# Weaving two GEMMs and the attention of the next batch step by step, with all tails on 128 rows

## Chip, cores and metric

The kernel runs on one core of a Trainium2 chip. The metric is the device time in microseconds (us). TensorE (PE) does the matmuls, VectorE (DVE) and ScalarE (ACT) read its results out of the PSUM banks (an eviction), and GpSimd (POOL) issues the input loads.

## The reference

For each of 8 batches, a Nystrom attention runs over 8 heads of 576 tokens and 64 features, followed by two GEMMs with a squared relu between them.

```python
q_lm, k_lm = segment means of q, k        # 32 segments of 18 tokens
A, Bm, C = softmax(q k_lm^T), softmax(q_lm k_lm^T), softmax(q_lm k^T)
for _ in range(6): Z = 2 * Z - Z @ Bm @ Z # Newton, 32x32 per head
x = A @ Z @ C @ v                         # per head, heads joined: 4608 x 512
out = relu(x @ w_in)**2 @ w_out           # 512 -> 2048 -> 512
```

The kernel folds Z, C, v and w_in into one matrix G per batch. The first GEMM is therefore A times G ("mlp_in", 64 matmuls of 288 columns a batch), and the second is "mlp_out" (576 matmuls of 512 columns in all). The products that make G are called W products below. The first W product of a batch marks the end of its attention.

## The kernel before

576 tokens are four chunks of 128 and a tail of 64. Before, each tail is a matmul whose stationary operand has 64 rows:

```python
for c in range(NC4 + 1):
    r = P if c < NC4 else TAIL                      # 128, or 64 for the tail
    nc.tensor.matmul(means[:, (1 - ti) * NPAIR + p, :],
        lhsT=X[nm][0:r, c, 2*p:2*p+2, :].rearrange("p h d -> p (h d)"),
        rhs=seg[0:r, c, :], start=(c == 0), stop=(c == NC4))
# ... the same pattern in the transposes of q, k and A, and in C times v
```

`batch_loads` loads q, k and v of a batch and copies q and k into another layout on VectorE. Batch 1 is loaded after w_out. The list scheduler of the language orders the instructions of each engine before the run, by its own estimate of when data is ready. The engines then keep that order.

```python
loaded[0] = batch_loads(0)           # ... w_in, constants, w_out (cut) ...
loaded[1] = batch_loads(1)
# inside batch_loads:
nc.vector.tensor_copy(nat[:, 0:NC4, :, :], raw.rearrange("p h c d -> p c h d"))
# main loop
res = {0: attention(0)}
for b in range(B):
    if b + 2 < B: loaded[b + 2] = batch_loads(b + 2)
    if b + 1 < B: res[b + 1] = attention(b + 1)
    mlp_in(b, *res.pop(b), gT)
    for t in tiles_of(b): mlp_out(b - b % 2, t, gT)   # same batch; one PSUM bank "o"
```

The Newton loop ran the two groups of four heads one after the other. It had separate copies and updates of 128 and 256 columns for each.

The softmax here doesn't subtract the row's maximum and nothing guards it: scores larger than these inputs give would overflow.

Of the kernel before, what the change touches and what calls it, by code (L numbers as in the profile page):

```python
# [8 lines left out]
P = 128  # L9
# [7 lines left out]
B = 8  # L17
H = 8
S = 576
D = 64  # L20
# [13 lines left out]
def kernel(  # L34
# [15 lines left out]
    small = ctx.enter_context(tc.tile_pool(name="small", bufs=3))  # L50
    newt = ctx.enter_context(tc.tile_pool(name="newt", bufs=4))
# [6 lines left out]
    def batch_loads(b: int):  # L58

        X = {}  # L60
        for nm, src in (("k", k), ("q", q)):
            raw = loads.tile([P, H, NC4, D], BF16, tag="raw")
            nat = loads.tile([P, NC4 + 1, H, D], BF16, tag=nm + "nat")
            nc.gpsimd.dma_start(
                raw[:], src[b, :, 0:NC4 * P, :].rearrange("h (p c) d -> p h c d", c=NC4)
            )
            nc.gpsimd.dma_start(
                nat[0:TAIL, NC4, :, :], src[b, :, NC4 * P:S, :].rearrange("h p d -> p h d")
            )
            nc.vector.tensor_copy(  # L70
                nat[:, 0:NC4, :, :], raw.rearrange("p h c d -> p c h d")
            )
            X[nm] = nat
        vm = loads.tile([P, H, NC4, D], BF16, tag="vm")
        vt = loads.tile([P, H, D], BF16, tag="vt")
        nc.gpsimd.dma_start(
            vm[:], v[b, :, 0:NC4 * P, :].rearrange("h (p c) d -> p h c d", c=NC4)
        )
        nc.gpsimd.dma_start(
            vt[P - TAIL:P, :, :], v[b, :, NC4 * P:S, :].rearrange("h p d -> p h d")  # L80
        )
        X["vm"], X["vt"] = vm, vt
        return X

    loaded = {}
    loaded[0] = batch_loads(0)
    for j in range(4):
        nc.gpsimd.dma_start(
            w_in_bf[:, :, j * 512:(j + 1) * 512],
            moe_w_in[:, j * 512:(j + 1) * 512].rearrange("(kt cp) f -> cp kt f", cp=P),  # L90
        )

    ident_bf = const.tile([P, P], BF16, name="ident_bf")
    make_identity(nc, ident_bf[:])
# [5 lines left out]
    seg_f = const.tile([P, NC4 + 1, M], F32, name="seg_f")  # L100
# [3 lines left out]
    band(seg_f[:, NC4, :], [[-SEG, M]], NC4 * P, 1)  # L104
    band(seg_f[:, NC4, :], [[SEG, M]], SEG - 1 - NC4 * P, -1)
    seg = const.tile([P, NC4 + 1, M], BF16, name="seg")
    nc.vector.tensor_copy(seg[:], seg_f[:])  # L107

# [8 lines left out]

    bds = []
    for i in range(2):
        bd_t = const.tile([P, 2 * NPAIR, 2 * M], BF16, name="bd%d" % i)  # L120
        nc.vector.memzero(bd_t[:])
        bds.append(bd_t)
    EA = const.tile([P, 2, NC4 + 1, P], F32, name="EA")
    nc.vector.memset(EA[:, :, NC4, :], 1.0)

    for j in range(4):
        nc.gpsimd.dma_start(
            w_out_bf[:, 4 * j:4 * j + 4, :],
            moe_w_out[512 * j:512 * j + 512, :].rearrange("(ft fp) c -> fp ft c", fp=P),
        )  # L130
    loaded[1] = batch_loads(1)

    def acol(b, c):

        if b % 2 == 0:
            return c * P
        return 0 if c == NC4 else TAIL + c * P

    def attention(b: int):
        X = loaded.pop(b)  # L140
        BD = bds[b % 2]

        means = psum.tile([P, 2 * NPAIR, M], F32, tag="n", bufs=3)
        for ti, nm in enumerate(("k", "q")):
            for p in range(NPAIR):
                for c in range(NC4 + 1):
                    r = P if c < NC4 else TAIL
                    nc.tensor.matmul(  # L148
                        means[:, (1 - ti) * NPAIR + p, :],
                        lhsT=X[nm][0:r, c, 2 * p:2 * p + 2, :].rearrange("p h d -> p (h d)"),  # L150
                        rhs=seg[0:r, c, :],
                        start=(c == 0), stop=(c == NC4),
                    )
        nc.scalar.copy(BD[0:64, :, 0:M], means[0:64, :, :])
        nc.vector.tensor_copy(BD[64:128, :, M:2 * M], means[64:128, :, :])
        STk = small.tile([P, NPAIR, M], BF16, tag="STk")
        nc.scalar.copy(STk[:], means[:, NPAIR:2 * NPAIR, :])

        bm = psum.tile([P, 2, M], F32, tag="n", bufs=3)
        for p in range(NPAIR):  # L160
            nc.tensor.matmul(bm[64 * (p % 2):64 * (p % 2) + 64, p // 2, :],
                             lhsT=BD[:, p, :], rhs=STk[:, p, :], start=True, stop=True)
        Eb = small.tile([P, 2, M], F32, tag="Eb")
        nc.scalar.activation(Eb[:], bm[:], AF.Exp, scale=SCALE)
        rs = small.tile([P, 2], F32, tag="rs")
        nc.vector.reduce_sum(rs[:], Eb[:], axis=AX.X)
        rr = small.tile([P, 2], F32, tag="rr")
        nc.vector.reciprocal(rr[:], rs[:])
        Bn = small.tile([P, 2, M], F32, tag="Bn")
        nc.vector.tensor_tensor(Bn[:], Eb[:], rr[:, :].unsqueeze(2).to_broadcast([P, 2, M]),  # L170
                                ALU.mult)
        BnT = small.tile([P, 2, M], F32, tag="BnT")
        nc.vector.transpose(BnT.rearrange("p a m -> p (a m)"), Bn.rearrange("p a m -> p (a m)"))
        colps = psum.tile([P, 2, M], F32, tag="n", bufs=3)
        nc.tensor.matmul(colps.rearrange("p a m -> p (a m)"),
                         lhsT=blk.rearrange("p a m -> p (a m)"),
                         rhs=Bn.rearrange("p a m -> p (a m)"), start=True, stop=True)
        n1 = small.tile([P, 2], F32, tag="n1")
        nc.vector.reduce_max(n1[:], colps[:], axis=AX.X)
        c1 = small.tile([P, 2], F32, tag="c1")  # L180
        nc.vector.tensor_scalar(out=c1[:], in0=n1[:], scalar1=1e-6, scalar2=None, op0=ALU.add)
        rc = small.tile([P, 2], F32, tag="rc")
        nc.vector.reciprocal(rc[:], c1[:])

        def spread(t, qd):
            return t[:, qd, :].unsqueeze(1).to_broadcast([P, 4, M])

        sts, BTs = [], []
        for qd in range(2):
            BT = small.tile([P, 4, M], BF16, tag="BT")  # L190
            nc.vector.tensor_tensor(BT[:], spread(BnT, qd), blk[:], ALU.mult)
            st = newt.tile([P, 2, 4, M], BF16, tag="st")
            nc.vector.scalar_tensor_tensor(out=st[:, 0, :, :], in0=spread(BnT, qd),
                                           scalar=rc[:, qd:qd + 1], in1=blk[:],
                                           op0=ALU.mult, op1=ALU.mult)
            nc.vector.scalar_tensor_tensor(out=st[:, 1, :, :], in0=spread(Bn, qd),
                                           scalar=rc[:, qd:qd + 1], in1=blk[:],
                                           op0=ALU.mult, op1=ALU.mult)
            BTs.append(BT.rearrange("p a m -> p (a m)"))
            sts.append(st.rearrange("p z a m -> p (z a m)"))  # L200


        T = {}
        for nm in ("q", "k"):
            tT = attn.tile([P, NPAIR, S], BF16, tag=nm + "T", bufs=1)
            for p in range(NPAIR):
                tps = psum.tile([P, S], BF16, tag="n", bufs=3)
                for c in range(NC4 + 1):
                    r = P if c < NC4 else TAIL
                    nc.tensor.transpose(  # L210
                        tps[:, c * P:c * P + r],
                        X[nm][0:r, c, 2 * p:2 * p + 2, :].rearrange("p h d -> p (h d)"),
                        ident_bf[0:r, 0:r],
                    )
                if p % 2 == 0:
                    nc.vector.tensor_copy(tT[:, p, :], tps[:])
                else:
                    nc.scalar.copy(tT[:, p, :], tps[:])  # L218
            T[nm] = tT


        EC = attn.tile([P, 2, NC4, P], BF16, tag="EC")
        ECt = attn.tile([P, 2, P], BF16, tag="ECt")
        for nm, slot0 in (("q", NPAIR), ("k", 0)):
            for qd in range(2):
                sc = psum.tile([P, NC4, P], F32, tag="n", bufs=3)
                for i in range(2):
                    p = 2 * qd + i
                    for c in range(NC4):
                        nc.tensor.matmul(sc[:, c, 64 * i:64 * i + 64],  # L230
                                         lhsT=T[nm][:, p, c * P:c * P + P],
                                         rhs=BD[:, slot0 + p, :], start=True, stop=True)
                dst = EA[:, qd, 0:NC4, :] if nm == "q" else EC[:, qd, :, :]
                nc.scalar.activation(dst, sc[:], AF.Exp, scale=SCALE)  # L234
        tl = psum.tile([P, 2, P], F32, tag="n", bufs=3)
        for nm, slot0, r0 in (("q", NPAIR, 0), ("k", 0, P - TAIL)):
            for p in range(NPAIR):
                nc.tensor.matmul(tl[r0:r0 + TAIL, p // 2, 64 * (p % 2):64 * (p % 2) + 64],
                                 lhsT=T[nm][:, p, NC4 * P:S],
                                 rhs=BD[:, slot0 + p, :], start=True, stop=True)  # L240
        nc.scalar.activation(EA[0:TAIL, :, NC4, :], tl[0:TAIL, :, :], AF.Exp, scale=SCALE)
# [168 lines left out]
```

## Time and profile before

The median of the runs is 398.1 us.

The first view is the page of the kernel before: span, busy time of each engine, then TensorE and its granted clock in 40 slices, in tenths.

```profile
span 397.2 us, 6929 instructions
...
PE 345.4 (87%) x2768; PEld 195.7 (49%) x2768; DVE 213.7 (54%) x524; ACT 170.0 (43%) x377; POOL 46.2 (12%) x68
...
PE   0440679999999999999999999999999999999985
...
PEclk9999999999999999999999999999999999999999
```

TensorE looks full after the start, but overlapping matmuls count as busy. The Trainium skill ("Perfetto Trace Analysis", Identifying the Most-Contended Engine) says that matmul busy time is not a good measure of the distance to the limit. So I count matmuls instead. Back to back, a 512-column matmul starts every 216 ns, a 288-column one every 122 ns, a 128-column one every 56 ns.

The second view is the chain of work that ended last (start, duration in us, what). Only the first W products of batches are kept, without those of batches 2 and 3.

```profile
58.72 1.96 PE g L326 x6
...
95.63 0.77 PE g L326 x6
...
220.87 0.77 PE g L326 x6
...
264.99 0.77 PE g L326 x6
...
306.30 0.77 PE g L326 x6
...
350.42 0.77 PE g L326 x6
```

The first batch is through at 58.7 us. Steady batches then take 41.3 and 44.1 us in turn.

The third view is the timeline of the start, with the idle time before an instruction and what ended it in brackets.

```profile
37.68 0.69 DVE L70 COPY nat<-raw 128x2048 bf16<-128x2048 bf16 x1 [16.21 <-DMA raw<-in_k_dram]
38.29 0.81 DVE L216 COPY tT<-tps 128x576 bf16<-128x576 bf16 x2
...
38.79 1.44 PE L230 MATMUL sc<-bd_120,tT 128*128 128x64 bf16 x24 [14.18 <-DVE tT L216]
```

VectorE stood 16 us before the copy of batch 1's k. Batch 0's own transposed q and k stood behind that copy, so TensorE waited 14.2 us for them.

The fourth view is the timeline around fifteen transposes of a steady batch. Three of them are 64-row tails, which the timeline merges with the others.

```profile
197.09 1.44 PE L210 MATMUL tps<-ident_bf,nat 128*128 128x128 bf16 x15
...
198.46 0.66 PE L342 MATMUL h<-AT,G 128*128 128x288 bf16 x4
```

Fifteen transposes take 1.37 us from first start to the next group. At 56 ns each they would take 0.84 us.

The fifth view is TensorE's waits longer than 0.15 us (engine, line, what it waited for: us in total, times, longest).

```profile
PE sc L230 <- DVE tT L216: 14.2, 1, 14.2
PE means L148 <- DVE seg L107: 12.8, 1, 12.8
PE ops L352 <- DVE o_sb L358: 4.9, 8, 0.8
```

The first is the wait for the transposed q and k. The second, for a constant, comes before any data is there. The third is the wait for the single output bank of the second GEMM.

### The profile page before, as it was taken

The numbers are of one execution on the slowest core, as the hardware profiler recorded it, in microseconds if no ns is written. First come the engines' busy times: TensorE is split into PE (matmuls) and PEld (weight loads), VectorE is DVE, ScalarE is ACT, GpSimd is POOL, SyncE is SP. The second block draws the span as 40 slices with busy tenths as digits, with TensorE's granted clock in tenths as the row PEclk, the third lists the DMA queues.
The fourth block names the chain that finished last, engine by engine and source line by source line (L and its number), as shares of the span: only waits on it lengthen the run. The fifth ranks groups of instructions, "written<-read, shape, count | busy, mean of one in ns | idle before, by whom it ended". The sixth has DMA issues, their size and how long they took to land.

```text
span 397.2 us, 6929 instructions
## 1 busy us (share of the span) xinstructions
PE 345.4 (87%) x2768; PEld 195.7 (49%) x2768; DVE 213.7 (54%) x524; ACT 170.0 (43%) x377; POOL 46.2 (12%) x68
## 2 busy tenths in 40 slices
PE   0440679999999999999999999999999999999985
PEld 0330334754565455654565456545655556645532
DVE  1311744787179714893489426972578236952500
ACT  1020404772178313852385225832584129633500
POOL 8431220111011100210030101010000000000000
PEclk9999999999999999999999999999999999999999
DMA  9999994195228521916154613043000010002021
GB/s 105 198 206 199 189 113 57 10 111 83 59 40 108 56 85 54 103 18 115 53 56 66 100 48 58 4 45 95 28 2 22 32 54 29 2 26 81 0 79 54
DMA packets 47136, 28.23 MB, mean 71 GB/s; under 512 B 13824, under 2 KB 42496, under 8 KB 47104
## 3 DMA queue, kind: packets, MB, share of 16 engines
q0 software_dynamic: 41856, 18.35, 37.9%
q1 hardware_dynamic: 5248, 9.44, 6.4%
q8 instruction: 21, 0.34, 0.4%
q14 instruction: 11, 0.09, 0.1%
HBM read 36.70 MB, written 9.44 MB: 116 GB/s over the span
## 4 chain that ended last, share of the span: by engine, by line
PE 70%; DMA 10%; ACT 9%; DVE 4%; issue 4%; POOL 2%; DVEq 0%; ACTq 0%; POOLq 0%
PE ops L352 31%; PE h L342 15%; DMA raw<-in_q_dram 7%; PE tps L210 6%; PE g L326 5%; PE means L148 4%; DMA w_in_bf<-in_moe_w_in_dram 4%; PE cv L300 3%; ACT r L346 3%; PE nt L253 2%; DVE stn L259 2%; DVE o_sb L358 2%; ACT EA L234 2%; ACT EC L234 2%; PE tps L285 2%
## 5 line engine op out<-in xcount | busy, mean ns | idle before, releaser
L352 PE MATMUL ops<-w_out_bf,gT 128*128 128x512 bf16 x576 | 148.3, 381 | 6.3 <-DVE o_sb L358 4.9
L342 PE MATMUL h<-AT,G 128*128 128x288 bf16 x512 | 92.3, 292 | 2.4 <-ACT r L346 1.6
L346 ACT ACTIVATE r<-h 128x576 bf16<-128x576 f32 x128 | 81.3, 658 | 12.5 <-PE h L342 11.9
L352 PEld LDWEIGHTS <-gT 128*128 128x128 bf16 x576 | 53.6, 98 | 65.3 <-issue 17.8
L347 DVE TENSOR_TENSOR gT<-r 128x576 bf16<-128x576 bf16 x128 | 55.0, 450 | 16.5 <-ACT r L346 15.6
L342 PEld LDWEIGHTS <-G 128*128 128x128 bf16 x512 | 44.8, 98 | 20.8 <-issue 8.4
L358 DVE COPY o_sb<-ops 128x512 f32<-128x512 f32 x20 | 13.8, 692 | 65.6 <-PE ops L352 65.0
L331 ACT CAST G<-g 128x512 bf16<-128x512 f32 x32 | 18.1, 587 | 51.9 <-PE g L326 51.9
L210 PE MATMUL tps<-ident_bf,nat 128*128 128x128 bf16 (+1 forms) x320 | 33.4, 225 | 0.1
L148 PE MATMUL means<-seg,nat 128*128 128x32 bf16 (+1 forms) x320 | 22.4, 184 | 12.8 <-DVE seg L107 12.8
L252 ACT CAST U<-nt 128x128 bf16<-128x128 f32 x96 | 23.5, 269 | 18.8 <-PE nt L250 17.7
L218 ACT COPY tT<-tps 128x576 bf16<-128x576 bf16 x32 | 20.4, 638 | 24.5 <-PE tps L210 24.5
L356 ACT COPY o_sb<-ops 128x512 f32<-128x512 f32 x16 | 9.4, 586 | 47.1 <-PE ops L352 30.3
L333 DVE CAST G<-g 128x512 bf16<-128x512 f32 x32 | 22.1, 692 | 13.5 <-PE g L326 13.5
L210 PEld LDWEIGHTS <-nat 128*128 128x128 bf16 (+1 forms) x320 | 24.4, 102 | 9.9 <-issue 1.6
L148 PEld LDWEIGHTS <-nat 128*128 128x128 bf16 (+1 forms) x320 | 18.1, 99 | 19.7 <-DVE nat L70 8.3
L70 DVE COPY nat<-raw 128x2048 bf16<-128x2048 bf16 x16 | 11.6, 737 | 28.4 <-DMA raw<-in_k_dram 22.1
L259 DVE SCALAR_TENSOR_TENSOR stn<-stn,nt 128x256 bf16<-128x256 bf16 x64 | 24.8, 417 | 1.4 <-ACT U L252 0.5
L250 PE MATMUL nt<-stn,BT 128*128 128x128 bf16 x80 | 17.9, 224 | 5.9 <-DVE stn L259 3.7
L326 PE MATMUL g<-w_in_bf,WT 128*64 128x512 bf16 x128 | 21.7, 421 | 0.5 <-DVE WT L318 0.5
L253 PEld LDWEIGHTS <-U 128*128 128x128 bf16 x96 | 9.3, 97 | 21.8 <-ACT U L252 17.5
L230 PEld LDWEIGHTS <-tT 128*128 128x128 bf16 x256 | 10.8, 101 | 16.4 <-issue 15.1
(138 smaller groups left out, 341.4 us busy)
## 6 DMA issues: line engine op xcount, KB each, us to landing
out_dram<-o_sb SPq DMA_DIRECT2D x32, 256.0 KB, 2.3
raw<-in_k_dram POOLq DMA_DIRECT2D x8, 512.0 KB, 6.1
raw<-in_q_dram POOLq DMA_DIRECT2D x8, 512.0 KB, 7.9
vm<-in_v_dram POOLq DMA_DIRECT2D x8, 512.0 KB, 6.3
w_in_bf<-in_moe_w_in_dram POOLq DMA_DIRECT2D x4, 512.0 KB, 13.7
w_out_bf<-in_moe_w_out_dram POOLq DMA_DIRECT2D x4, 512.0 KB, 17.7
out_dram<-o_sb SPq DMA_DIRECT2D x8, 128.0 KB, 3.9
nat<-in_k_dram POOLq DMA_DIRECT2D x8, 64.0 KB, 3.2
```

Source lines behind the costliest of these rows:

```text
L148: nc.tensor.matmul(means[:, (1 - ti) * NPAIR + p, :], lhsT=X[nm][0:r, c, 2 * p:2 * p + 2, :].rearrange("p h d -> p (h d)"), rhs=seg[0:r, c ...
L210: nc.tensor.transpose(tps[:, c * P:c * P + r], X[nm][0:r, c, 2 * p:2 * p + 2, :].rearrange("p h d -> p (h d)"), ident_bf[0:r, 0:r],)
L218: nc.scalar.copy(tT[:, p, :], tps[:])
L252: nc.scalar.copy(U[:], nt[:, 0:P])
L259: nc.vector.scalar_tensor_tensor(out=stn[:], in0=st, scalar=2.0, in1=nt[:, P:3 * P], op0=ALU.mult, op1=ALU.subtract)
L326: nc.tensor.matmul(g[64 * i:64 * i + 64, :], lhsT=WT[:, 2 * qd + i, :], rhs=w_in_bf[:, 2 * qd + i, n * 512:n * 512 + 512], start=True, sto ...
L333: nc.vector.tensor_copy(dst, g[:])
L342: nc.tensor.matmul(h[:, j, 0:HALF], lhsT=G[:, qd, f * P:(f + 1) * P], rhs=AT[:, qd, j * HALF:(j + 1) * HALF], start=(qd == 0), stop=(qd == 1))
L346: nc.scalar.activation(r.rearrange("p (j t) -> p j t", j=2), h[:, :, 0:HALF], AF.Relu)
L347: nc.vector.tensor_tensor(gT[:, f, o:o + S], r[:], r[:], ALU.mult)
L352: nc.tensor.matmul(ops[:], lhsT=gT[:, f, t * P:t * P + P], rhs=w_out_bf[:, f, :], start=(f == 0), stop=(f == NF - 1))
L358: nc.vector.tensor_copy(o_sb[:], ops[:])
```

## The change

The change makes the attention a generator that yields after every step. Each first-GEMM unit is followed by a step of attention and a few matmuls of the second GEMM, which lags one batch. Tails of q and k share one 128-row chunk. Zero rows in the constants stand in for the missing half. Both Newton groups go through one copy and one update, with scores, row sums and C values woven between. Batch 1 is loaded ahead of w_out. The layout copies of q and k move from the load helper, called for batch 1 ahead of batch 0's attention, to the head of their own batch's attention. The tiles of the last second GEMM alternate between two banks. The core of the diff:

```diff
-            nat = loads.tile([P, NC4 + 1, H, D], BF16, tag=nm + "nat")
+        X["qkt"] = loads.tile([P, H, D], BF16, tag="qkt", name="qkt")
+        for nm, src, r0 in (("k", k, TAIL), ("q", q, 0)):   # k rows 64..127, q rows 0..63
...
-                    r = P if c < NC4 else TAIL
-                        lhsT=X[nm][0:r, c, 2 * p:2 * p + 2, :].rearrange("p h d -> p (h d)"),
-                        rhs=seg[0:r, c, :],
+                    src = nat[nm][:, c, 2*p:2*p+2, :] if c < NC4 else X["qkt"][:, 2*p:2*p+2, :]
+                        rhs=seg[:, c + (ti if c == NC4 else 0), :],
...
+    load_qk(1, loaded[1])
+    load_v(1, loaded[1])
     for j in range(4):                                      # w_out
...
-    loaded[1] = batch_loads(1)
...
+            nc.scalar.copy(U[:], nu[:])                     # both groups, 256 columns
+            yield
+            if side: side.pop(0)(); yield                   # scores, tails, A rows, C values, A^T
...
+        for u in range(2 * NF):
+            if u % 2 == 0: mlp_in(b, u // 2, AT, G, gT)
+            else: advance(tiles, per)                       # mlp_out of batch b - 1
+            advance(att, want - done)                       # attention of batch b + 1
```

## The prediction

> **What bounds it now.** One core, full clock throughout (clock row 9s). The overview gives TensorE 345 of 397 us busy, but matmuls overlap there, so I counted start-to-start times in the timeline. Back to back a 128x512 matmul takes 216 ns, 128x288 takes 122, 128x128 takes 56, 64 columns 29, 32 columns 25. The Trainium skill ("TensorE: Matmul & The Clock Gate", Part 1) gives N/2.4 GHz + 2.5 ns; the trace agrees. Charging each matmul that, one batch needs about 33 us of TensorE (second GEMM 15.5, first GEMM 7.8, attention about 10), 34 with the pairs of 64-column products of the W step. By the chain, a steady batch takes 41.3 and 44.1 us in turn (265 to 350 us), mean 42.7, so some 8.5 us per batch are not streaming. About 3.7 of these are the 64-row matmuls: a 128-row transpose costs 56 ns, one followed by a 64-row one 152, and leaving it 132; segment means pay 108 and 119 instead of 25. The rest is Newton waits (ACT copy, DVE update), waits for the eviction of the single output bank (6.3 us in all, groups view) and column-group switches.
>
> The start is latency: first means at 12.8 us, TensorE idle 14.2 us (waits view: scores on DVE copy), because a DVE copy of batch 1's k stands in front and its load lands at 37.5 us, behind w_out. First W product at 58.7 us, second batch's at 95.6. After the last attention: 43.6 us, partly ACT-bound.
>
> **What the change does.**
> 1. 64-row matmuls go (shared tail chunk, zero rows elsewhere). Worth 3.7 us x 6 to 7 batches on the path: 22-26 us.
> 2. Batch 1's q, k, v load ahead of w_out. The program order still puts batch 1's copies in front of batch 0's Newton updates on DVE. From before's landings (about 0.185 MB/us) k1 lands near 26, q1 near 30 us, so the 14 us wait nearly vanishes. Means still start near 12.3 us, as the mask cast stands behind q's copy. With A rows, C values and transposes inside the Newton chain, first W product near 38.5 us.
> 3. Stage 0 (attention 1 with first GEMM alone) is latency- and DVE-bound: DVE about 27 us of work. Second W product near 69 us (before 95.6).
> 4. Stages 1-6: PE 34 us. Stalls I expect left: between U product and its consumers the order holds 0.5-0.9 us of other TensorE work in several iterations, against about 0.8 us for the ACT copy plus queueing; output bank turnover about 0.3-0.8 us a tile; DVE near 75-80% occupied. I take 3 us of stalls: 37 us a batch, 222 us.
> 5. Stage 7 (first GEMM 7 with second GEMM 6): 23.5 us. Final second GEMM with alternating banks: 5 x 3.45 + 4 drain = 21.5.
>
> Sum 69 + 222 + 23.5 + 21.5 = 336 span, plus 1.4 us as before: 337.
>
> **Prediction: 337 us, 8 in 10 between 324 and 351. Faster by over 2%: 0.97; within 2%: 0.02; slower: 0.01.**
>
> **What would show it.** No 64-row groups; transposes 56 ns apart throughout; first W product 36-41 us; second 65-72; a period of 35-39 us; in the waits view Newton waits and output-bank waits dominate; the last second GEMM alone from about 314 us.
>
> **What would make it wrong.** The DVE queue (row reduce and normalise of A, 1.5 us each) stalling every Newton update: period 40, total 355. Batch 1's loads late: start 10 us longer. Weaving hiding everything: period 34.5, total 322.

## The result, and the profile after

The changed kernel takes 326.7 us (median of 4 runs, 326.4 to 327.3) against 398.1 us. All outputs are right. The ratio is 0.821, with a 95% interval of 0.819 to 0.823. A ratio is the mean time of one kernel's runs over that of the other's of the same rounds, so it is not quite the ratio of the medians.

The page of the changed kernel, same parts:

```profile
span 324.8 us, 6593 instructions
...
PE 292.1 (90%) x2662; PEld 180.7 (56%) x2704; DVE 207.5 (64%) x457; ACT 165.8 (51%) x313; POOL 46.8 (14%) x70
...
PE   0385599999999999999999999999999999999994
...
PEclk9999789999999999999999999999999999999999
```

The chain of the changed kernel, first W products of the batches, without those of 4 and 5:

```profile
39.00 1.96 PE n L381 x8
...
67.36 0.84 PE n L381 x6
...
95.18 0.83 PE n L381 x6
...
130.96 0.77 PE n L381 x5
...
237.73 0.82 PE n L381 x6
...
273.61 0.77 PE n L381 x5
```

The first batch is through at 39.0 us, 19.7 us earlier, and a steady batch takes 35.7 us ((273.61 - 130.96) / 4) instead of 42.7 ((350.42 - 179.55) / 4; batch 3's first W product came at 179.55 us).

VectorE's timeline at the start of the changed kernel shows batch 1's copy again in front of batch 0's work:

```profile
28.26 0.69 DVE L154 COPY nat<-raw 128x2048 bf16<-128x2048 bf16 x1 [3.30 <-DMA raw<-in_k_dram]
28.87 0.68 DVE L350 SCALAR_TENSOR_TENSOR st<-st,n 128x512 bf16<-128x512 bf16 x1
```

It stands further back, in front of batch 0's third Newton update, and costs VectorE 3.3 us instead of 16.2.

TensorE's timeline, one group of transposes at the start and one in a steady batch:

```profile
13.22 1.01 PE L178 MATMUL n<-ident_bf,nat 128*128 128x128 bf16 x8
...
212.68 0.61 PE L178 MATMUL n<-ident_bf,nat 128*128 128x128 bf16 x8
213.13 1.03 PE L416 MATMUL ops<-w_out_bf,gT 128*128 128x512 bf16 x4
```

In the steady batch eight transposes take 0.45 us, 56 ns each, with no 64-row matmul among them. Eight at 13 us lie 106 ns apart, although the page's clock row shows a 9 there. I come back to that.

TensorE's waits in the changed kernel:

```profile
PE n L161 <- DVE seg L106: 12.1, 1, 12.1
PE n L333 <- DVE st L350: 4.8, 6, 3.1
PE n L343 <- ACT U L336: 1.6, 5, 0.5
...
PE ops L416 <- ACT o_sb L422: 0.8, 3, 0.4
```

**One account for all kernels.** I split each profiled span into four parts. "First W" is the time of the first W product. "Needed" adds up all later matmuls of the built program at their back-to-back rate (216 ns for 512 columns, 216 for a pair of W products, 122 for 288, 109 for 256, 56 for 128, 29 for 64, 25 below). "Over" is what TensorE took beyond that, up to its last matmul. The remainder, 4 us, is the last copy and store. "Needed" takes its counts from the program, so records missing from a trace don't distort it. The median is of all runs, the other columns are of the one profiled execution.

| kernel | median us | first W | needed | over |
|---|---|---|---|---|
| before | 398.1 | 58.7 | 258.1 | 76.2 |
| before_load1 | 397.3 | 58.2 | 258.1 | 75.3 |
| before_pool12 | 390.1 | 42.9 | 258.1 | 82.7 |
| before_rows128 | 366.9 | 57.9 | 258.6 | 44.2 |
| no_lag | 343.9 | 38.7 | 258.2 | 41.1 |
| rows64_all | 343.1 | 39.5 | 257.9 | 40.3 |
| plain_order | 341.7 | 38.8 | 258.3 | 38.8 |
| lag_only | 336.6 | 39.0 | 258.5 | 32.2 |
| wout_first | 330.4 | 42.4 | 258.3 | 22.8 |
| early9 | 329.0 | 40.7 | 255.3 | 27.2 |
| early18 | 329.0 | 50.5 | 253.5 | 18.9 |
| **changed kernel** | 326.7 | 39.0 | 258.3 | 23.4 |
| qk1_first | 324.8 | 36.5 | 258.3 | 24.2 |
| early18p | 322.2 | 43.6 | 253.5 | 20.0 |

The needed work did not shrink. The change took 19.7 us from the start and 52.8 us from "over". The experiments ask which part of the change did which.

### The profile page after: what moved, and what is told of

The parts are those of the page before. It is cut to its first block, busy times and chain, and to the rows that moved or that the text cites. A ratio compares the mean times of both kernels' runs of the same rounds, so it can differ in the third digit from the quotient of the medians.

```text
span 324.8 us, 6593 instructions
## 1 busy us (share of the span) xinstructions
PE 292.1 (90%) x2662; PEld 180.7 (56%) x2704; DVE 207.5 (64%) x457; ACT 165.8 (51%) x313; POOL 46.8 (14%) x70
## 4 chain that ended last, share of the span: by engine, by line
PE 74%; DVE 9%; DMA 5%; ACT 5%; POOL 3%; issue 3%; DVEq 0%; POOLq 0%; ACTq 0%
PE ops L416 33%; PE h L400 16%; PE n L381 6%; DMA raw<-in_k_dram 5%; PE n L311 3%; PE n L161 2%; PE n L333 2%; PE n L343 2%; PE n L266 2%; PE n L178 2%; ACT r L404 2%; DVE nat L154 2%; DVE gT L405 1%; PE n L346 1%; DVE T L185 1%
## 5 line engine op out<-in xcount | busy, mean ns | idle before, releaser
L404 ACT ACTIVATE r<-h 128x576 bf16<-128x576 f32 x128 | 83.4, 656 | 59.3 <-PE h L400 58.7
L350 DVE SCALAR_TENSOR_TENSOR st<-st,n 128x512 bf16<-128x512 bf16 x40 | 27.3, 682 | 10.6 <-PE n L346 10.3
L388 DVE CAST G<-n 128x512 bf16<-128x512 f32 x32 | 21.6, 689 | 11.4 <-PE n L381 11.4
L336 ACT CAST U<-n 128x256 bf16<-128x256 f32 x48 | 18.4, 382 | 20.2 <-PE n L333 19.8
L386 ACT CAST G<-n 128x512 bf16<-128x512 f32 x32 | 18.4, 588 | 12.8 <-PE n L381 12.8
L381 PE MATMUL n<-w_in_bf,WT 128*64 128x512 bf16 x128 | 21.7, 416 | 0.7 <-DVE WT L373 0.5
L187 ACT COPY T<-n 128x1024 bf16<-128x1024 bf16 x16 | 15.9, 1015 | 9.5 <-PE n L178 9.5
L178 PE MATMUL n<-ident_bf,nat 128*128 128x128 bf16 x256 | 20.7, 230 | 0.0
L333 PE MATMUL n<-st,BT 128*128 128x128 bf16 x96 | 13.9, 228 | 5.9 <-DVE st L350 4.8
L178 PEld LDWEIGHTS <-nat 128*128 128x128 bf16 x256 | 17.6, 104 | 1.5
L343 PE MATMUL n<-st,U 128*128 128x128 bf16 x96 | 16.8, 229 | 1.8 <-ACT U L336 1.6
L161 PEld LDWEIGHTS <-nat 128*128 128x128 bf16 x256 | 9.7, 97 | 13.5 <-DVE nat L154 8.2
```

The costliest lines, as they stand in the source:

```text
L161: nc.tensor.matmul(means[:, ti, p, :], lhsT=src.rearrange("p h d -> p (h d)"), rhs=seg[:, c + (ti if c == NC4 else 0), :], start=(c == 0), ...
L178: nc.tensor.transpose(tps[:, i, c, :], nat[nm][:, c, 2 * p:2 * p + 2, :].rearrange("p h d -> p (h d)"), ident_bf[:],)
L333: nc.tensor.matmul(nu[:, qd, :], lhsT=BT[:, qd, :], rhs=st[:, 0, qd, :], start=True, stop=True)
L336: nc.scalar.copy(U[:], nu[:])
L343: nc.tensor.matmul(nv[:, 1, qd, :], lhsT=U[:, qd, :], rhs=st[:, 1, qd, :], start=True, stop=True)
L350: nc.vector.scalar_tensor_tensor(out=stn.rearrange("p z q n -> p (z q n)"), in0=st.rearrange("p z q n -> p (z q n)"), scalar=2.0, in1=nv.r ...
```

## The experiments

### The 64-row tails, undone and done alone

**rows64_all** is the changed kernel with 64-row tails again. q's and k's tails are loaded to rows 0 to 63 of two tiles.

```diff
-   src = nat[nm][:, c, ...] if c < NC4 else X["qkt"][:, ...]
+   src = nat[nm][:, c, ...] if c < NC4 else X[nm + "t"][0:TAIL, ...]
-   nc.tensor.transpose(tps[:, o:o + P], an[:, qd, c, :], ident_bf[:])
+   nc.tensor.transpose(tps[:, o:o + r], an[0:r, qd, c, :], ident_bf[0:r, 0:r])
-   lh, rv = ect[:, qd, :], X["vt"][:, ...]
+   lh, rv = ect[TAIL:P, qd, :], X["vt"][TAIL:P, ...]   # and 8 tail transposes of 64 rows for 4 of 128
```

> The changed kernel with the tails of q, k, A and C back on 64 rows (means, tail transposes, A's transposes, C values), all else as it is. The 8 tail transposes of a batch stand in a row here, so they change the row mode only once. Theory (the cost is the switch into and out of 64-row mode, about 0.17 us a pair of switches): 8 means, 2 A transposes and 2 C groups pay, about 2.1 us a batch, so 12 to 18 us longer in all, 339 to 345 us; in the trace 64-row after 64-row starts within 40 ns. Rival 1 (each 64-row matmul costs that much): the 8 transposes pay too, 24 us or more. Rival 2 (the woven TensorE has slack that hides it): under 5 us.

It took 343.1 us, 16.4 more than the changed kernel, and the steady batch 37.9 us instead of 35.7. The timeline shows where a 64-row matmul costs:

```profile
222.72 0.26 PE L162 MATMUL n<-seg,nat 128*128 128x32 bf16 x4
222.91 0.19 PE L162 MATMUL n<-seg,kt 64*128 64x32 bf16 x1
223.02 0.27 PE L162 MATMUL n<-seg,nat 128*128 128x32 bf16 x4
...
231.68 0.20 PE L251 MATMUL n<-ident_bf,qt 64*128 64x64 bf16 x1
231.72 0.19 PE L251 MATMUL n<-ident_bf,kt 64*128 64x64 bf16 x1
231.75 0.19 PE L251 MATMUL n<-ident_bf,qt 64*128 64x64 bf16 x1
```

A means matmul in front of a 64-row one costs 108 ns, and the 64-row one 119, where two of 128 rows cost 25 each. The pair of switches costs 0.18 us. The tail transposes, 64 rows after 64 rows, start 29 ns apart. So the cost is the switch and not the half-filled array, as the theory said, and rival 1 falls. The Trainium skill ("TensorEngine Tiling (Array Packing)", Key Properties) says that a change of tiling mode drains TensorE. The trace shows no drain as such, but it shows that the change costs time, and how much. Eight means, two A transposes and two C groups make the 2.2 us a batch, some 15 of the 16.4 us. About 1 us more is a stretch at half clock (75.8 to 79.2 us) that the changed kernel's profile lacks.

**before_rows128** is the kernel before with the shared tail chunk and zero rows. The load order, Newton chain and loop stay.

```diff
-   lhsT=X[nm][0:r, c, ...], rhs=seg[0:r, c, :]
+   src = X[nm][:, c, ...] if c < NC4 else X["qkt"][:, ...]
+   lhsT=src, rhs=seg[:, c + (1 - ti if c == NC4 else 0), :]
-   nc.tensor.transpose(tps[:, c * P:c * P + r], X[nm][0:r, c, ...], ident_bf[0:r, 0:r])   # 8 tails
+   nc.tensor.transpose(tps[:, p, :], X["qkt"][:, ...], ident_bf[:])                       # 4, q and k together
-   nc.tensor.transpose(tps[...], an[0:r, qd, c, :], ident_bf[0:r, 0:r])
+   nc.tensor.transpose(tps[...], an[:, qd, c, :], ident_bf[:])
-   lh, rv, on = ECt[lo:P, qd, :], X["vt"][lo:P, ...], ones_bf[lo:P, :]
+   lh, rv, on = ECt[:, qd, :], X["vt"][:, ...], ones_bf[:]        # zero rows 0 to 63
```

> The kernel before with only the shared tail chunk and zero rows, so that all matmuls but the W products, the W-transposed pieces and the small 64-column ones have 128 rows; order, loads and Newton chain as before. Theory: the 64-row switches were on the path, 3.5 to 3.7 us a batch, so 22 to 28 us shorter, 370 to 376 us, and the batch period falls from 42.7 to about 39. Rival: TensorE waits for the Newton chain anyway and the time freed turns into waits: under 12 us.

It took 366.9 us, 31.0 less, more than the 22 to 28 expected. The batch period fell from 42.7 to 38.65 us. That is 4.05 us a batch, 24 us over the six steady batches. Before, the tail transposes stood one by one between 128-row ones, so ten transposes of a batch pay too. Twenty switches at 0.18 us make 3.6 of the 4.05 us. The edit also turns the eight score matmuls of the tails, which write 64 columns side by side, into four of 128. In the kernel before, the way into these eight and out of them takes 257 and 129 ns where 122 and 29 are usual, so I estimate 0.2 us a batch for that. The rest is open.

The other 7 us lie between the first two W products (36.8 to 29.6 us). Most of that is TensorE's clock. The trace's own clock records begin with full speed at 71.4 us in the kernel before and at 56.6 us here. In the changed kernel they show full speed from 33.2 to 36.6 us, and for good from 43.4 us. Ahead of that, two W products take 425 ns instead of 216. From 58.7 to 71.4 us the kernel before ran at half rate, which cost 12.7 / 2, about 6.3 us (an estimate). The Trainium skill ("TensorE: Matmul & The Clock Gate", What's actually happening) describes the half-rate state and its release after a sustained busy stretch of about 3.4 us. The rates of 106 and 56 ns agree with it. Why the kernel before was released only after 12 busy us is not settled. The tails alone don't decide it: before_load1 (below) has them too and its records begin with full speed at 62.6 us. So I count only the 24 us of the steady batches as gain of the 128 rows.

### The start

**before_load1** is the kernel before with `loaded[1] = batch_loads(1)` moved ahead of the w_out loads.

```diff
+    loaded[1] = batch_loads(1)
     for j in range(4):                                      # w_out
...
-    loaded[1] = batch_loads(1)
```

> The kernel before with only batch 1's loads put ahead of w_out. Theory (load order makes half of the gain of the start): batch 1's k lands near 28 instead of 37.5 us, TensorE's 14.2 us wait shrinks to about 4 to 6, first W product at 48 to 50 us instead of 58.7, 8 to 11 us shorter in all, 387 to 390 us. Rival (the landing was only the label of another wait): under 4 us.

It gained nothing: 397.3 us. Batch 1's k did land at 27 instead of 37.5 us. But the scheduler now placed the copy further ahead in VectorE's queue. It stood in front of the copy of batch 0's means, near the head of its work:

```profile
27.27 0.69 DVE L70 COPY nat<-raw 128x2048 bf16<-128x2048 bf16 x1 [14.27 <-DMA raw<-in_k_dram]
27.99 0.43 DVE L155 CAST bd<-means 64x256 bf16<-64x256 f32 x1
...
28.77 0.29 PE L161 MATMUL bm<-STk,bd 128*64 128x32 bf16 x4 [12.92 <-ACT STk L157]
```

The wait is nearly as long as before (12.9 us of TensorE's time against 14.2) and lies 10 us earlier, with nearly all of batch 0's work behind it. The theory, which was also a step of the prediction, fell.

**before_pool12** leaves the load order alone and moves the copies of batches 1 and 2 to GpSimd:

```diff
-            nc.vector.tensor_copy(
+            (nc.gpsimd if b in (1, 2) else nc.vector).tensor_copy(
```

> The kernel before with one thing moved: the layout copies of batches 1 and 2 run on GpSimd instead of VectorE, the load order stays (w_out first). Loading batch 1 earlier alone had gained nothing, because the scheduler then put the copies even further ahead in the VectorE queue. Theory (the start's wait is the place of copies that wait for a load in VectorE's in-order queue, ahead of batch 0's own work, not the load's lateness): the 14.2 us wait and the later ones for batch 2's copies go, first W product at 41 to 45 us instead of 58.7; in all 8 to 17 us shorter, less if the copies are slow on GpSimd and hold batch 1. Rival (attention of batch 0 is bound by something else): first W product later than 52 us.

The first W product came at 42.9 us, 15.8 earlier, so the place in the queue was the cause. In all it gained only 7 us (390.1 against 397.1 in the same rounds, ratio 0.982, interval 0.980 to 0.985), just under the 8 to 17 expected. The stretch to the second W product grew from 36.8 to 43.3 us. The same fault came back there: the copies of batch 3, still on VectorE, waited for their loads in front of batch 1's first Newton update, and TensorE waited 3.2 us for that. Its half-rate time in that stretch was also 3.6 us longer, which makes 1.8. A copy took 1.9 us on GpSimd, and while one ran there, at 56.1 us, a VectorE product that takes 0.22 us elsewhere took 1.91.

```profile
38.09 1.89 POOL L70 COPY nat<-raw 128x2048 bf16<-128x2048 bf16 x1 [14.52 <-DMA raw<-in_k_dram]
...
42.94 1.96 PE L326 MATMUL g<-w_in_bf,WT 128*64 128x512 bf16 x8 [0.52 <-DVE WT L318]
...
67.54 0.69 DVE L70 COPY nat<-raw 128x2048 bf16<-128x2048 bf16 x1 [3.44 <-DMA raw<-in_k_dram]
...
72.47 0.74 DVE L259 SCALAR_TENSOR_TENSOR stn<-st,nt 128x256 bf16<-128x256 bf16 x2
```

**wout_first** is the changed kernel with w_out loaded ahead of batch 1 again.

```diff
-    load_qk(1, loaded[1])
-    load_v(1, loaded[1])
     for j in range(4):                                      # w_out
...
+    load_qk(1, loaded[1])
+    load_v(1, loaded[1])
```

> The changed kernel with w_out loaded ahead of batch 1's q, k, v, as in the kernel before. The order listing shows that the copies of batch 1's k and q move behind batch 0's last Newton update on VectorE, in front of its last products. Theory (the load order shortens the start through the VectorE queue): batch 1's k lands near 37.5 us as before, first W product at 42 to 49 us instead of 39.0, 4 to 10 us longer in all. Rival (the gain of the start comes from the restructured attention, not from the load order): first W product within 2 us of 39.

330.4 us, first W product at 42.4 us, 3.4 later and 3.7 us longer in all, at the lower end of the theory and just below it. The copy of k now stands behind batch 0's fifth Newton update, in front of its last one, and that of q in front of the copy of WT. TensorE waits 5.6 and 2.7 us there:

```profile
PE n L369 <- DVE zt L357: 5.6, 1, 5.6
PE n L333 <- DVE st L350: 3.8, 5, 2.0
PE n L381 <- DVE WT L373: 2.7, 1, 2.7
```

So of the 19.7 us at the start, the load order decides 3 to 4. The rest comes from where the copies stand and from a shorter attention. With no copy of batch 1 on VectorE, the old attention still needs 42.9 us to the first W product (before_pool12); the new one needs 36.5 with little waiting left (qk1_first, below). So I estimate some 6 us for the new attention. About 1 us of that could be the clock, which was at full speed there from 32.5 to 35.9 us, when TensorE had 0.9 us of matmuls. Why the copies land in a better place was not tested. The diff shows a plain candidate: the kernel before writes batch 1's copies ahead of batch 0's attention, the changed kernel writes them after it. I tried another, the single buffer of the copied layout. A build of the changed kernel with two buffers for k had the same VectorE order, so it was not run.

**qk1_first** loads batch 1's k and q ahead of w_in too.

```diff
     load_v(0, loaded[0])
+    load_qk(1, loaded[1])
     for j in range(4):                                      # w_in
...
-    load_qk(1, loaded[1])
     load_v(1, loaded[1])
```

> The changed kernel with batch 1's k and q loaded ahead of w_in as well. In the trace of the change TensorE waits 3.1 us for a Newton update that stands behind the copy of batch 1's k, which waits for its load until about 28 us. Theory: that wait goes, w_in still lands before the first W product (near 33 us), first W product at 35.5 to 37.5 us, 1.5 to 3.5 us shorter than the change, 323 to 325.5 us. Rival: w_in lands late and the W products wait, no gain or longer.

324.8 us, 1.9 less, first W product at 36.5 us. The theory held, with a gain at its lower end. The two kernels ran in different rounds; against the kernel before, which ran beside each, the ratios are 0.817 and 0.821 and their intervals touch. The earlier first W product is sure, the size of the gain is not.

### The weave and the lag

**no_lag** keeps the weave. Each stage runs 16 units of the first GEMM and then the second GEMM of the same batch:

```diff
-        tiles = mlp_out(b - 1, prev) if b else iter(())
+        tiles = mlp_out(b, gT)
-            if u % 2 == 0:
-                mlp_in(b, u // 2, AT, G, gT)
+            if u < NF:
+                mlp_in(b, u, AT, G, gT)
```

> The changed kernel with the second GEMM of batch b in the second half of stage b instead of one batch later; attention of the next batch still woven through the stage. Theory: without the lag the first half of a stage is bound by ScalarE (a relu takes 0.66 us, its four matmuls 0.49 us), 1 to 2 us a batch, and the last stage too; the first stage gets work to fill it, which gives some back: 3 to 12 us longer, 330 to 338 us. Rival: the scheduler smooths it out, within 2 us.

343.9 us, 17 more, a miss of the expected 3 to 12 us. The reason given was wrong too. TensorE waited 0.4 us in all for a relu. Instead it waited once in every batch for the normalised A rows, and for the single output bank:

```profile
PE n L299 <- DVE an L291: 9.2, 8, 1.4
PE n L333 <- DVE st L350: 3.7, 4, 2.7
PE ops L416 <- ACT o_sb L422: 3.1, 7, 0.6
...
PE ops L416 <- DVE o_sb L424: 1.5, 7, 0.2
```

In the second half of such a stage the only filler (independent work for TensorE during a wait) is the second GEMM. All its tiles share one bank, which ScalarE and VectorE empty in turn, and VectorE also makes the A rows (1.48 us each for the row sums and the normalising). In the changed kernel the "an" wait occurs once, in batch 0. These waits are 11.6 us longer here than in the changed kernel, where "over" is 17.7 us larger. What makes the rest was not traced.

**plain_order** has neither lag nor weave: attention, first GEMM and second GEMM are written one after the other, with the new attention.

```diff
-        for u in range(2 * NF):                             # the woven loop
...
+        for _ in att: pass
+        for f in range(NF): mlp_in(b, f, AT, G, gT)
+        for _ in mlp_out(b, gT): pass
```

> The changed kernel with attention of the next batch, first GEMM and second GEMM written one after the other as in the kernel before (no lag, no weaving in the program), and the new attention (merged Newton, side steps inside it, 128 rows, load order) kept. Theory: the written weave keeps TensorE fed through the Newton chain, so 10 to 25 us longer, 337 to 352 us. Rival: the list scheduler interleaves by itself, and the structure of the attention steps is what counts: under 6 us longer.

341.7 us, 15 more, as the theory said, but this run drops the lag as well and cannot tell the two apart. **lag_only** has the lag without the weave.

```diff
-        for u in range(2 * NF):                             # the woven loop
...
+        for _ in att: pass
+        for f in range(NF): mlp_in(b, f, AT, G, gT)
+        for _ in (mlp_out(b - 1, prev) if b else iter(())): pass
```

> The changed kernel with the second GEMM one batch late as in the change, but attention of the next batch, first GEMM and the late second GEMM written one after the other, not woven. The two earlier runs without the lag (woven 343.9 us, unwoven 341.7) have the same batch period of about 38.5 us against 35.7 of the change. Theory (the lag alone gives the gain, as it makes filler that depends on nothing in the stage; the list scheduler then places it): period 35 to 36.5, 325 to 332 us. Rival (lag and weave only together): 335 to 343 us, the period near 38.

336.6 us, within the rival's range, though the mean period of the later batches, 36.6 us, lies nearer to the theory's. With the table this gives a two-by-two of "over":

| over, us | no weave | weave |
|---|---|---|
| no lag | 38.8 | 41.1 |
| lag | 32.2 | 23.4 |

The weave alone costs 2.3 us, the lag alone gains 6.6, and both together gain 15.4. By the medians it is 2.2, 5.1 and 15.0; lag_only's runs spread over 2.7 us. The step from before_rows128 to plain_order, 5.4 us of "over", is the new attention with all else that these two differ in, such as the alternating banks at the end. No run separates these.

### Trying for more

**early9** and **early18** start from qk1_first and let the first nine or eighteen steps of batch 1's attention run inside batch 0's.

```diff
-    for _ in attention(0, R):
-        pass
+    att1, ahead = attention(1, R), 0
+    for n, _ in enumerate(attention(0, R)):
+        if n >= 14 and ahead < 9:        # 18 in early18
+            advance(att1, 1); ahead += 1
```

> The changed kernel with batch 1's k and q loaded ahead of w_in (324.8 us measured), and the first nine steps of attention of batch 1 (means, transposes, Newton's start) woven into the second half of attention of batch 0. In the change the stretch between the first two W products takes 28.4 us for 21.2 us of TensorE work, the worst of all stages. Theory: about 3 us of TensorE work and the head of the chain move into idle time at the start; first W product 1 to 3 us later, second 3 to 6 us earlier; 320 to 323.5 us. Rival: VectorE is full in that stretch, no gain (324 to 327 us).

> As the one with nine steps, but eighteen, so that four of the Newton half steps of batch 1 run beside batch 0's chain. Theory: more of the chain is hidden, 318 to 323 us. Rival: the two chains fight for VectorE and the three shared output banks and delay the first W product by as much, 324 to 328 us.

Both took 329.0 us, a miss, and beyond the rivals' ranges too. The rival named the right direction but not the cause. VectorE was not full in early18, it stood still:

```profile
47.91 0.69 DVE L154 COPY nat<-raw 128x2048 bf16<-128x2048 bf16 x1 [6.82 <-DMA raw<-in_k_dram]
48.52 0.68 DVE L350 SCALAR_TENSOR_TENSOR st<-st,n 128x512 bf16<-128x512 bf16 x1
```

A copy of batch 2's k, not yet loaded, stood in front of a Newton update. In early9 the same copy waited 7.0 us in front of evictions of batch 0's W products, and TensorE waited 5.7 us for them. **early18p** is early18 with batch 2's copies on GpSimd:

```diff
-            nc.vector.tensor_copy(nat[nm][:], X[nm + "raw"].rearrange(...))
+            (nc.gpsimd if b == 2 else nc.vector).tensor_copy(nat[nm][:], ...)
```

> As the run with eighteen steps woven early (329.0 us), with batch 2's layout copies on GpSimd instead of VectorE. In that run VectorE sat idle for 6.8 us at 41 us, with batch 0's last Newton update behind a copy of batch 2's k whose load had not landed. Theory (the loss of both early runs was that copy's place in the queue, not VectorE being full): the 6.8 us wait goes, first W product at 42 to 45 us, second at 63 to 66, 319 to 323 us in all, 1 to 5 us shorter than the kernel with batch 1's k and q first (324.8). Rival (the two chains fight for VectorE and output banks): 325 us or more.

322.2 us (322.1 to 323.1, five runs), 6.7 less than early18, as the queue theory says. It beats both kernels: ratio 0.810 to the kernel before, where the changed kernel has 0.821. It is 1.4% under the changed kernel. Work worth 4.8 us of TensorE time moved ahead of the first W product (needed 253.5 instead of 258.3).

## Why the prediction was right or wrong

337 us was predicted, with 324 to 351 as range. 326.7 was measured, so the range held it and the sum was 10 us too long. Its opening, "full clock throughout", was a misreading: the page's row of 9s covers a stretch up to 71.4 us without clock records, in which W products ran at half rate. The predicted span parts were 69 + 222 + 45 = 336. Measured are 67.4 (second W product), 206.2 (to the last one) and 51.2 (end), 324.8 in all.

1. *64-row matmuls, 22 to 26 us.* Right in mechanism, and in size for the kernel before: 24 us in the steady batches when done alone, 31 in all. The clock state after the first W product, about 6 us, was not in the prediction at all. Undone in the changed kernel the tails cost 16.4 us, as eight of the ten transposes stand in a row there.
2. *"Batch 1's q, k, v load ahead of w_out ... so the 14 us wait nearly vanishes", first W product near 38.5.* The number was right (39.0), the cause mostly wrong, so part of the match is luck. The step that failed is the one from the earlier landing to the vanished wait. Done alone in the kernel before, the load order gained nothing. Undone in the changed kernel it cost 3.7 us. What counts is where a copy that waits for a load stands in VectorE's in-order queue (first W product 15.8 us earlier with the copies taken out of it), and some 6 us are the shorter attention, by estimate. The prediction had read the copy's place from the trace, and then gave the credit to the load.
3. *Second W product near 69 us.* Measured 67.4. The number was right. VectorE was busy for 23 of the 28.4 us, not 27, and the stage also ran 16 matmuls of the second GEMM that are written in the next one (such counts are from wout_first and qk1_first, which have the same order of stages and lost no record; the changed kernel's trace lost 42). Whether VectorE bounds it was not tested.
4. *Stages 1 to 6, 37 us each with 3 us of stalls, 222 us.* Mis-sized. The later periods were 35.5 to 35.8 us. With the W pairs charged as in the prediction (34 us), stalls were 1.5 to 1.8 us, about half of the 3 assumed. The expected waits between the U product and its consumers stayed at 1.6 us in all, and those for the output bank at 0.8. Besides, the first of these stages took only 27.8 us. It holds 24.6 us of needed TensorE time where the later ones average 33.3, since some of its second GEMM had run in the stage before and other work slipped into later stages.
5. *End, 45 us.* Measured 51.2. The end holds 160 matmuls of 512 columns where the program writes 144, and 76 of 288 where it writes 64: some 5 us of slipped work come back here. Stages and end together were 267 predicted and 257.4 measured. By estimate 3.5 us of the difference are the 16 matmuls that ran before these stages, and the rest is fewer stalls.

## What to carry to other kernels

Look at who stands behind a copy that waits for a load in an in-order queue before moving the load: an earlier load helps nothing if the scheduler then moves the copy ahead as well. Look for filler for a latency chain that does not depend on the stage it fills: weaving pays here only with a lag of one batch. Pad odd tails to the full row count with zero rows, or put the small ones side by side, so that the array changes its row mode once and not at every tail.

## What the Trainium skill lacked or had wrong

- "TensorEngine Tiling (Array Packing)", Key Properties, says that a mode switch drains TensorE but not what it costs: a switch from 128 to 64 rows and back cost 0.18 us (108 + 119 ns against 25 each for means; 152 + 132 ns against 56 each for transposes), and 64 after 64 rows cost nothing (29 ns apart).
- "TensorE: Matmul & The Clock Gate", Part 1: the two rates of 106 and 56 ns agree. I found no page that says that a clock summary can show full speed where no clock record exists yet. Here the profile page's row shows 9 at 13 us while transposes lay 106 ns apart. Nor does the skill page's busy window of about 3.4 us explain the kernel before, which was released only at 71.4 us after 12 us of W products and GEMM work.
- "PSUM — Partial Sum Buffer", Engine vs sequencer instructions, says that VectorE's queue is a strict FIFO, which agrees with all runs. I found no page that says how much a scheduler's place for a copy that waits on a load can cost: 16.2 us of VectorE's time before, 3.3 in the changed kernel, 6.8 in early18.
- "GPSIMD Engine Reference", Engine selection, calls one-input elementwise work on GpSimd "roughly line-rate" and gives no time for a layout copy. That of 128x2048 bf16 took 1.9 us there and 0.69 us on VectorE, so moving it costs a factor of 2.7 where it isn't hidden.
